# Attention and a gated feed-forward on one core: K and Q rows on every fourth partition, re-timed instruction orders, a shifted end

## The chip, the cores and the metric

The kernel runs on one core of a Trainium2 chip. The metric is the device time of one execution in microseconds. The engines are TensorE (PE, with its weight loads as PEld), VectorE (DVE), ScalarE (ACT), GpSimd (POOL) and the sync engine (SP), which here only issues DMAs.

## The reference

For `x` of 2048 tokens by 448, with 16 heads of width 28 and a hidden width of 1792:

```python
g = sigmoid((x * gate_w).sum(-1, keepdims=True))
# a: attention
q, k, v = split(x @ wqkv)                       # 16 heads, 28 wide
p = softmax(q @ k.T * 28 ** -0.5)
a = concat_heads(p @ v) @ wo
# b: gated feed-forward
gate, up = x @ W_gate, x @ W_up
b = ((gate * (gate > 0)) * up) @ W_down
return g * a + (1 - g) * b
```

All inputs and outputs are float32.

## The kernel before

Most matmuls work in float32r on operands that are split in two, a high part and a low rest (`act_high`, `dve_high` for the first, `low` on VectorE and `pool_low` on GpSimd for the second); products of the parts are added up in PSUM. Eight PSUM banks hold all results of TensorE.

**Projections.** The first 141 us project the tokens to Q, K and V and write them to DRAM (`qk_d`, `v_d`), Q and K as a high and a low plane.

**Heads.** For each head, `load_k` and `load_q` bring K and Q back into one of three buffers each. A buffer stacks four copies of 28 rows (high or low parts), 112 partitions in all, so that one matmul over 128 partitions gives the product of both parts of both sides; the last 16 partitions hold -1 on K's side and the row maxima (as high and low part) or zeros on Q's side. Row maxima are found first: `smax` (line 240) computes scores with queries on the partitions, VectorE takes the maximum (line 241). For three of a head's four blocks of queries (all four of the first head) the probabilities come from `scores` (line 263) with the exponential on ScalarE (line 265). The last block takes another way: `raw_scores` (line 271) copies the scores out, `raw_max` keeps a running maximum over keys, `raw_top` reduces it, writes it to DRAM (`mr_d`) and spreads it back to all partitions, `raw_less` subtracts it on GpSimd and `raw_exp` takes the exponential. `pv` (line 648) multiplies the probabilities with V in 64 matmuls at the end of a round.

**Rounds.** There are 32 rounds, two for each head. Each round's order on TensorE is a string written out ahead: `s` a score matmul, `m` a maximum, `r` a raw score, `x` a matmul of the feed-forward's gate and up part (line 610), each with the bank that it writes as a digit; `d` and `e` stand for a `raw_max` on VectorE and a `raw_exp` on ScalarE. `ROUNDS` lists which string each round uses: FIRST and SECOND for the first head, AA with BA or BB most of the time, DA with BC twice where the feed-forward goes on to another block of tokens, CA, CB, AY, BY, AZ and BZ at the end. A bank can be written again when its reader is done, so the spacing of equal digits in a string sets whether TensorE waits.

At the end of an odd round the sync queue gets, in this order: new blocks of tokens if they change (`X<-x_d`), K of head h+3, the write of `mr_d`, its broadcast (which waits until the write has landed), Q of head h+3, and the next weights of the feed-forward (`wgr<-wgu`). Transfers of one queue are issued in order. The first maximum of head h+3 comes in the following even round.

**Feed-forward.** Gate and up results are multiplied and spilled to DRAM (`h_d`). After the rounds, `down` multiplies them with W_down (line 899): step i reads h of block i, split into `HH` by `split_d`, and the weights `WD` that `split_d` splits too for the first 14 steps. `fetch_d` loads four steps ahead. Between the downs stands the attention's output: `fetch_o` loads the heads' results of a block of tokens into `or` (one buffer), `split_o` splits them in two halves on ScalarE and GpSimd, and `wout` (line 853) multiplies them with `wo`. The list at line 940 says before which down each of these stands.

Of the kernel before, what the change touches and what calls it, by code (L numbers as in the profile page):

```python
# [23 lines left out]
DH = 28  # L24
G = 4
GD = G * DH
# [19 lines left out]

FIRST = ("m2m3m6m7s0s1uxxxxs0xm2lxxs3xm6xUxs1xm7xs0m2xxm3xs1xxs0m7m2s1xr3r0r7m1xdr2xdr3xdxr1s0dxxdxxxm2m0s3xxm"
         "1xm3r2xxm0xdm1xxs3xs0xxm2r3s0m1xdxs2s0m1m2m0m1")  # L50

SECOND = ("xs0m1r2xs6m7dxs3xm0s1xm6s7xr3s2xm1dxs0m7xs6xm2s1r0xs3m6dxs7xm1s2xm3r7xs0xds2m1xs3m0xs7xm2r1s3xm0ds7x"
          "xs2m3xs0r1m2xs3dxm0xs2s3xm1xs2r0m3xs1dm2xxs3m1xs0xs3r2xm1s0dm3xxxs1m0s2xxm1xs2")

AA = ("xm0s1xr2m6s7xm3xs1xm2s7xr0m6xs1dxm3s7xm2xr6s1m0xdxs7m3xs2m1xr0exm7s3dxm2s1exm7xs3xm0er1xs2m3dxes7xm0"
      "xs2m3er1xxs0m2dxes3xxm0m2xes1r3xm0xxdes2m1xs0xem3s2xm1s0xm3r2xs1m0dxxxs1m0")

BB = ("xm0s1r2xm7s6dxxm3s1xm0xs7r6xm2s1dxm3xs0xm7r2s1xm6dxs0xm3xs7m1xr0s2xm3dxs7m1xs2xm3xr7m0s2xdxm1s3xm2s0"
      "xr3xm1s0dxm2xxs1m0s3xxr2m1s3xdm0xxs1m3s2xxm0r1s2m3xdxs0xm2xxs0m1")

BA = ("xs0m1r2s7xm6ds3xs0m1r7xs6m3ds0xr2s1m6xds3xm0s7xr1s6m3s2dxm7s0xr6s3m2xds1m0xs7r3xs2m1ds6xm7s0r2xs1m6d"
      "xs3m0xs7r1s6xm2ds7xm0xs6")

AY = ("xs0m1s2xr6m7s3m0s2xr6xm1s3ds7m2xm0s3xr1s7xm6ds3m2xs0r7s6xm3ds1m0xes2r6xs3m1xem7s2ds0xm1exr3s7m2s6xm0"
      "dexs1m2s7xem6s0xr3xm1s7m2r6ds0xs1m7d")

BY = ("xs0r1ds2xs6xs7xr3ds0s2xs6r1dexs7xs0r2dexs3xs6xs7r1dexs0xs3r2dexxs6r7ds1xs0s3xs2r6ds1xs0xs7xs2s1x")

AZ = ("xs0xs1xxs2xxs6xs7xxs3xs0xxs1xxs2xs7xxs3xs0xxs1xxs2xs3xxs0xxs1xs2exxs3xs0exxs1xxs2exs0xxs1xx")

BZ = ("xs0xs1xxs2xxs6xs7xxs3xs0xxs1xxs2exs7xxs3xes0xxs1xxes2xs3xxs0exxs1xs2xexs3xs0xxs1xxs2xs0xxs1xx")

DA = ("xs0m1xs2r6m7xm3xs0xm2xs6r1m7xs0dxm3xs6m2xr7s0xm1dxs6m3xxm2s0xr1m7s3xdm0xs2xm3xs7m1xr2s0xm7dxs3em1xs0"
      "xm3er2xxs0m1dxem3xs0xm1xes2r0xm3xxdes1m2xs3xm0es1xm2r3xes0m1dxs2xxs1m0m2")

BC = ("xm0s1r2xm7s6dxxm3s1xem0xs7r6xem2s1dxm3xs0exm7r2s1xm6dxs0xm3xs7m1xr0s2xm3dxs7m1xs2xm3xr7m0s2xdxm1s3xm"
      "2s0xr3xm1s0dxm2xxs1m0s3xxr2m1s3xdm0xxs1m3s2xxm0r1s2m3xdxs0xm2xxs0m1")

CA = ("xs0r1m2xs6m7xm3xs0m1xs6m2xr7xs0m3dxm6s1xxm2r0s3xm1dxs7xm6s2xm3xs1m7r0xs2xdm1s3xm7xer2s0xm3dxs1em7xs0"
      "m3xm1exs2m0xxem3r2s1xxdm0exxs3m1s2xexm0r3m2s1xdexs0xm1m2xes3m0xs1xm2xxr0m1s2d")  # L80

CB = ("xs0m1r2s7xm6ds3xm0s1r7exs6m3ds2xem1s0xr3m6s7xs2m1dxes0xr6m7s1xs2m3r0ds7xxm1s3ds2m6xxr7s1m3s0ds2m6xr1"
      "s3xm0ds7xm2s6xr0s7xm1ds6m2xs7")

ROUNDS = [FIRST, SECOND, AA, BA, AA, BB, AA, BA] + [DA, BC, AA, BA, AA, BB, AA, BA] * 2
ROUNDS += [CA, CB, CA, CB, AY, BY, AZ, BZ]

# [13 lines left out]
def gated_mix_kernel(ctx, tc, x, wq, wo, wgu, wd, out):  # L101
    nc = tc.nc
# [9 lines left out]
    def f32(ap):  # L112
        return ap.bitcast(F32)
# [37 lines left out]
    def act_high(dst, src):  # L151
        nc.scalar.activation(dst, src, AF.Copy)  # L152
# [4 lines left out]
    def low(dst, src, high):  # L157
        nc.vector.tensor_tensor(dst, src, f32(high), op=OP.subtract)  # L158
# [5 lines left out]
    qk_d = dram.tile([2, 2 * D, S], F32, name="qk_d")  # L164
# [19 lines left out]
    K = [vp.tile([P, S], F32R, name=f"K{r}") for r in range(3)]  # L184
# [27 lines left out]
    Q = {}  # L212

    def load_k(h):
        for r in range(4):
            nc.sync.dma_start(f32(K[h % 3])[DH * r:DH * (r + 1)], qk_d[r % 2, 2 * DH * h:2 * DH * h + DH, :])

    def load_q(h):
        Q[h] = QB[h % 3].rearrange("p j t -> p (j t)")
        for r in range(4):  # L220
            nc.sync.dma_start(f32(Q[h])[DH * r:DH * (r + 1)], qk_d[r // 2, 2 * DH * h + DH:2 * DH * (h + 1), :])

        n = P - GD if h < 3 else 2
        nc.sync.dma_start(f32(Q[h])[GD:GD + n], z_d[0:1].to_broadcast([n, S]))
# [79 lines left out]
    def xf(tb, b):  # L304
        return X[tb][b // 4][:, b % 4]
# [13 lines left out]
    with tc.tile_pool(name="qkv", bufs=1) as pa:  # L319
# [199 lines left out]
        split_w(*w4)  # L519
        w3 = load_w(3)  # L520
        load_k(0)
        load_q(0)

        units = [(qk, 3, 1), (qk, 2, 2), (qk, 3, 2)]
# [9 lines left out]
        for n, (f, *a) in enumerate(mixed):  # L534
# [3 lines left out]
            if n == 6:  # L538
                load_k(1)
                load_q(1)  # L540
# [5 lines left out]
            if n == len(mixed) - 7:  # L546
                load_k(2)
                load_q(2)
# [30 lines left out]
    done = sum(order.count("x") for order in ROUNDS) // 20  # L579
    SECOND = set(range(1, 2 * done, 2))  # L580
    PAIRED = SECOND | {k - 1 for k in SECOND}

    def lane(k):
        return slice(64 * k, 64 * k + 64)

    def split_f(i, high, low, part=(0, 1)):
# [7 lines left out]
        if part[-1] == 1:  # L594
            high(w[:, :, 6], wr[:, :, 3])
            for s in range(2):
                rows = lane(1 - (2 * i + s in SECOND))
                low(w[rows, s, 6], wr[rows, s, 3], w[rows, s, 6])
# [5 lines left out]
    def gu_mm(ps, i, s, n):  # L604
# [3 lines left out]
        if n == NT - 1 and 2 * i + s in PAIRED:  # L608
            rows = lane(int(2 * i + s in SECOND))
        nc.tensor.matmul(ps, WS[i][rows, s, a], xf(i // NF, b)[rows], start=(n == 0), stop=(n == NT - 1))  # L610
# [93 lines left out]
    for r, order in enumerate(ROUNDS):  # L704
        h, i0 = r // 2, 8 * r
# [15 lines left out]
        for o in re.findall("[a-zA-Z][0-9]?", order):  # L721
# [27 lines left out]
            elif o == "x":  # L749
                i, half, k = todo.pop(0)  # L750
# [124 lines left out]
    WD = pf.tile([P, NF, 2, D], F32R, name="WD")  # L875
# [9 lines left out]
    def split_d(i):  # L885
        if i < NF:
            r = DR.pop(i)
            early = i < 8
            (act_high if early else dve_high)(WD[:, i, 0], r)
            (low if early else pool_low)(WD[:, i, 1], r, WD[:, i, 0])  # L890
        HH[i] = pf.tile([P, 2, TB], F32R, name=f"hh_{i}", tag="hh", bufs=3)
        h = HK.pop(i)
        act_high(HH[i][:, 0], h)
        low(HH[i][:, 1], h, HH[i][:, 0])
# [38 lines left out]
    def before(i, *new):  # L933
        n = todo.index((down, i))
        todo[n:n] = new


    before(3, (normalise, H - 1))
    for tb, load, split, at in ((0, 3, (8, 9), (10, 11, 12, 13)), (1, 8, (12, 14), (17, 18, 19, 20)), (2, 21, (23, 25), (28,) * 4),
                                (3, 35, (37, 39), (42,) * 4)):  # L940
        before(load, (fetch_o, tb))
        for k, i in enumerate(split):
            n = todo.index((down, i))
            n -= todo[n - 1][0] is gate_up
            todo.insert(n, (split_o, tb, 2 * k))
        for t, i in enumerate(at):
            before(i, (wout, tb, t))
# [5 lines left out]
    for n, (f, *a) in enumerate(todo):  # L953
        if n in (7, 8):
            split_d(n - 7)
        if f is down:
            if a[0] + 4 < NB * NF:
                fetch_d(a[0] + 4)
            if a[0] + 2 < NB * NF:
                split_d(a[0] + 2)  # L960
        f(*a)
# [37 lines left out]
```

## Time and profile before

| | us |
|---|---|
| median of 3 executions | 1256.64 (1256.18 to 1258.26) |
| the profiled execution | 1257.98 |
| its span, first to last instruction | 1256.2 |

The profile shows one execution. Its busy time is per engine; matmuls overlap, so TensorE can look busy while it loses time. "line engine out<-in xcount | busy, mean | idle before, who ended it" is the form of a group; a row of the timeline is start, duration, engine, line and operation, with the idle time ahead of it in brackets and what ended it. Rows of SPq are DMA issues, not transfers. A wait that is put down to one DMA can belong to another on the same queue.

### The profile page before, as it was taken

To read this page: it belongs to the slowest core of one execution; us is meant where nothing else is said; L and a number is where in the kernel's file an instruction comes from. 1 tells how busy PE (TensorE), PEld (TensorE's weight loads), DVE (VectorE), ACT (ScalarE), POOL (GpSimd) and SP (SyncE) were. 2 spreads that over 40 slices of the span, in tenths; PEclk is the share of its full clock that TensorE was granted. 3 is DMA by queue.
4 is the path that set the end of the run, shared out by engine and by line. 5 is a ranking of instruction groups with operands and counts; after the bars stand their busy time and mean duration, and the time that the engine had idled before them with its cause. 6 is when DMAs were issued, how large, how long until landed. Compare 5 with 4: busy or idle time off the path is not lost.

```text
span 1256.2 us, 18815 instructions
## 1 busy us (share of the span) xinstructions
PE 1233.8 (98%) x6447; PEld 855.7 (68%) x6447; DVE 897.5 (71%) x1442; ACT 842.5 (67%) x1667; POOL 636.1 (51%) x708
## 2 busy tenths in 40 slices
PE   9999999999999999999999999999999999989998
PEld 6888766666656665666656666665565655989997
DVE  6488879787877877787878787878787734453342
ACT  5312677988788787978787888796877896422121
POOL 4232325573837483838293756646483677551020
PEclk9999999999999999999999999999999999999999
DMA  8986515151544343343535251526241122853432
GB/s 301 306 278 231 183 51 153 51 127 59 135 117 120 95 107 77 101 112 98 145 95 123 78 125 61 133 76 162 59 111 51 52 84 88 272 162 109 147 105 80
DMA packets 62035, 157.64 MB, mean 125 GB/s; under 512 B 12994, under 2 KB 19746, under 8 KB 57514
## 3 DMA queue, kind: packets, MB, share of 16 engines
q1 hardware_dynamic: 47924, 111.47, 32.3%
q0 software_dynamic: 13584, 44.52, 10.1%
q8 instruction: 50, 0.82, 0.3%
q10 hardware_dynamic: 432, 0.46, 0.1%
q14 instruction: 45, 0.37, 0.1%
HBM read 108.70 MB, written 48.16 MB: 125 GB/s over the span
## 4 chain that ended last, share of the span: by engine, by line
PE 72%; DMA 12%; ACT 6%; DVE 3%; POOL 2%; issue 2%; SPq 2%; ACTq 0%; DVEq 0%; POOLq 0%
PE b L610 15%; PE b L648 12%; PE b L240 11%; PE b L263 11%; PE b L899 9%; PE b L434 4%; DMA wgr<-wgu 4%; PE b L271 3%; ACT P L265 3%; PE b L452 3%; PE b L853 3%; DMA mr_d<-V 2%; DMA Q<-qk_d 1%; DMA K<-qk_d 1%; DMA V<-wq 1%
## 5 line engine op out<-in xcount | busy, mean ns | idle before, releaser
L241 DVE TENSOR_REDUCE mx<-b 128x1 f32<-128x512 f32 x784 | 522.9, 687 | 69.9 <-PE b L240 64.7
L265 ACT ACTIVATE P<-b 128x512 f32<-128x512 f32 x780 | 448.8, 608 | 140.1 <-PE b L263 129.5
L610 PE MATMUL b<-X,wg 128*128 128x512 f32 (+1 forms) x1232 | 429.2, 399 | 0.0
L240 PE MATMUL b<-K,Q 128*128 128x512 f32 x784 | 310.7, 400 | 10.9 <-DMA wgr<-wgu 7.3
L263 PE MATMUL b<-Q,K 128*128 128x512 f32 x784 | 312.0, 400 | 2.2 <-ACT P L265 1.9
L610 PEld LDWEIGHTS b<-X,wg 128*128 128x128 f32 (+1 forms) x1232 | 219.6, 188 | 60.7 <-issue 22.2
L648 PE MATMUL b<-P,v 128*32 128x512 f32 x1800 | 226.2, 594 | 0.0
L240 PEld LDWEIGHTS b<-K,Q 128*128 128x128 f32 x784 | 146.1, 188 | 62.9 <-ACT P L265 21.8
L263 PEld LDWEIGHTS b<-Q,K 128*128 128x128 f32 x784 | 147.0, 188 | 54.6 <-ACT P L265 24.2
L632 POOL DMA_DIRECT2D h_d<-rl x56 | 31.5, 564 | 281.2 <-DVE rl L626 234.0
L298 POOL TENSOR_TENSOR P<-P,V 128x512 f32<-128x512 f32 x120 | 150.7, 1291 | 43.4 <-DMA V<-mr_d 43.4
L298 POOL TENSOR_TENSOR V<-V 128x512 f32<-128x512 f32 x120 | 150.8, 1290 | 19.9 <-DMA V<-mr_d 19.9
L161 POOL TENSOR_TENSOR wg<-wgr,wg 128x384 fp32r<-128x384 f32 x216 | 155.5, 734 | 9.6 <-DVE wg L155 1.0
L648 PEld LDWEIGHTS b<-P,v 128*32 128x32 f32 x1800 | 61.7, 110 | 144.5 <-issue 143.4
L279 DVE TENSOR_TENSOR V<-b,V 128x512 f32<-128x512 f32 x215 | 145.9, 679 | 1.8 <-ACT V L275 1.3
L899 PE MATMUL b<-WD,hh 128*128 128x448 f32 x672 | 139.5, 368 | 0.0
L899 PEld LDWEIGHTS b<-WD,hh 128*128 128x128 f32 x672 | 127.5, 190 | 10.3
L152 ACT ACTIVATE hh<-hr 128x512 fp32r<-128x512 f32 x56 | 35.3, 631 | 122.5 <-PE b L899 107.0
L648 PE MATMUL b<-V,v 128*32 128x512 f32 x248 | 110.1, 593 | 0.0
L271 PE MATMUL b<-Q,K 128*128 128x512 f32 x240 | 97.3, 407 | 0.2
L158 DVE TENSOR_TENSOR hh<-hr,hh 128x512 fp32r<-128x512 f32 x56 | 49.2, 880 | 64.3 <-ACT hh L152 64.3
L434 PE MATMUL b<-X,W 128*128 128x512 f32 x280 | 76.0, 395 | 0.6 <-DVE K L158 0.6
(102 smaller groups left out, 1121.5 us busy)
## 6 DMA issues: line engine op xcount, KB each, us to landing
wgr<-wgu SPq DMA_DIRECT2D x55, 512.0 KB
K<-qk_d SPq DMA_DIRECT2D x64, 224.0 KB
Q<-qk_d SPq DMA_DIRECT2D x64, 224.0 KB
h_d<-rl POOLq DMA_DIRECT2D x56, 256.0 KB, 2.9
hr<-h_d SPq DMA_DIRECT2D x56, 256.0 KB
qk_d<-st POOLq DMA_DIRECT2D x21, 512.0 KB, 5.0
X<-x_d SPq DMA_DIRECT2D x24, 256.0 KB
x_d<-X POOLq DMA_DIRECT2D x5, 1024.0 KB, 5.6
```

The lines of the kernel that those rows point to most:

```text
L161: nc.gpsimd.tensor_tensor(dst, src, f32(high), op=OP.subtract)
L240: nc.tensor.matmul(ps, Q[h][:, u * P:(u + 1) * P], K[h % 3][:, c * TB:(c + 1) * TB], start=True, stop=True)
L241: nc.vector.tensor_reduce(MX[h][:, 4 * u + c:4 * u + c + 1], ps, axis=AX.X, op=OP.max)
L263: nc.tensor.matmul(ps, K[h % 3][:, kt * P:(kt + 1) * P], Q[h][:, j * TB:(j + 1) * TB], start=True, stop=True)
L265: nc.scalar.activation(prob(i, j), ps, AF.Exp, scale=SCALE)
L271: nc.tensor.matmul(ps, K[h % 3][:, kt * P:(kt + 1) * P], Q[h][:, 3 * TB:], start=True, stop=True)
L279: nc.vector.tensor_tensor(run, ps, run if i % NK > 1 else prob(i - 1, 3), op=OP.max)
L298: nc.gpsimd.tensor_tensor(own, own, piece(TOP), op=OP.subtract)
L434: nc.tensor.matmul(ps, W[:, a, c * P:(c + 1) * P], xf(tb, b), start=(n == 0), stop=(n == NT - 1))
L610: nc.tensor.matmul(ps, WS[i][rows, s, a], xf(i // NF, b)[rows], start=(n == 0), stop=(n == NT - 1))
L648: nc.tensor.matmul(po[32 * j:32 * j + 32], VH[h][:, i % NK], prob(i, j), start=(i == i0), stop=(i == i0 + ni - 1))
L899: nc.tensor.matmul(ACC[i // NF][t][:, :D], HH[i][:, a, t * P:(t + 1) * P], WD[:, f, b], start=(f == 0 and n == 0), stop=(f == NF - 1 and n ...
```

## The change

Three things change.

1. K and Q rows. Row d of copy r goes to partition 4d + r, where it went to 28r + d. The four transfers for K and for Q stay four, with 28 rows of 8 KB each.
2. Eleven of the thirteen orders are permuted (AZ and BZ are not). Each keeps its number of every letter.
3. The end. `split_d` puts the high part of all fourteen W_down blocks on ScalarE and the low part on VectorE; before, blocks 8 to 13 had their high part on VectorE and the low part on GpSimd. The first block's `split_o` stand before downs 9 and 10 (8 and 9 before) and its four `wout` before downs 12, 12, 13 and 13 (10, 11, 12 and 13 before).

```diff
-AA = ("xm0s1xr2m6s7xm3xs1xm2s7xr0m6xs1dxm3s7xm2xr6s1m0xdxs7m3xs2m1xr0exm7s3dxm2s1exm7xs3xm0er1xs2m3dxes7xm0"
-      "xs2m3er1xxs0m2dxes3xxm0m2xes1r3xm0xxdes2m1xs0xem3s2xm1s0xm3r2xs1m0dxxxs1m0")
+AA = ("xm0s1xr2m6s7xm3xs1xm2s0xr7m6xs1dxm3s0xm2xr6s1xm7dxs0m3xs2m1xr7exm0s2dxm3s1exxm0s2xr7em1s3xdm2xes0xm1"
+      "xs3xexm2r0s1m3xdexs2xm1s3xexm0r2m1s3xdexm0xxs3em1s2xxm0s3xm1s2xm0xxr1s2m0d")
...
     def load_k(h):
+        k = f32(K[h % 3])[:GD].rearrange("(d r) t -> r d t", r=4)
         for r in range(4):
-            nc.sync.dma_start(f32(K[h % 3])[DH * r:DH * (r + 1)], qk_d[r % 2, 2 * DH * h:2 * DH * h + DH, :])
+            nc.sync.dma_start(k[r], qk_d[r % 2, 2 * DH * h:2 * DH * h + DH, :])
 
     def load_q(h):
         Q[h] = QB[h % 3].rearrange("p j t -> p (j t)")
+        q = f32(Q[h])[:GD].rearrange("(d r) t -> r d t", r=4)
         for r in range(4):
-            nc.sync.dma_start(f32(Q[h])[DH * r:DH * (r + 1)], qk_d[r // 2, 2 * DH * h + DH:2 * DH * (h + 1), :])
+            nc.sync.dma_start(q[r], qk_d[r // 2, 2 * DH * h + DH:2 * DH * (h + 1), :])
...
             r = DR.pop(i)
-            early = i < 8
-            (act_high if early else dve_high)(WD[:, i, 0], r)
-            (low if early else pool_low)(WD[:, i, 1], r, WD[:, i, 0])
+            act_high(WD[:, i, 0], r)
+            low(WD[:, i, 1], r, WD[:, i, 0])
...
-    for tb, load, split, at in ((0, 3, (8, 9), (10, 11, 12, 13)), (1, 8, (12, 14), (17, 18, 19, 20)), (2, 21, (23, 25), (28,) * 4),
+    for tb, load, split, at in ((0, 3, (9, 10), (12, 12, 13, 13)), (1, 8, (12, 14), (17, 18, 19, 20)), (2, 21, (23, 25), (28,) * 4),
                                 (3, 35, (37, 39), (42,) * 4)):
```

The other ten changed orders are rewritten in the same way as AA.

More of the change, by code (lines that the diff above doesn't have):

```diff
@@ L43 @@
 AHEAD = 100
[L49 to L53, printed above, removed]
-AA = ("xm0s1xr2m6s7xm3xs1xm2s7xr0m6xs1dxm3s7xm2xr6s1m0xdxs7m3xs2m1xr0exm7s3dxm2s1exm7xs3xm0er1xs2m3dxes7xm0"
-      "xs2m3er1xxs0m2dxes3xxm0m2xes1r3xm0xxdes2m1xs0xem3s2xm1s0xm3r2xs1m0dxxxs1m0")
@@ L58 @@
[L58 to L67, printed above, removed]
+FIRST = ("m2m3m6m7s0s1uxxxxs0xm2lxxxxUs3xxs6s1m7xm0xs2m3xs1m7xxm2xxr0r1r3xm7s2dxr0dxxr7ds2xr1dxr3xs2dxr0dxxxdm"
+         "2s1xm3xxm0s1xm2xm3xm1s0xxm2xm3s0xm1xs2m0m2m1m0")
@@ new lines @@
+SECOND = ("xs0r1m2s6xm7dxs3xs0m2r6xs7m3dxs1xm0xs2m7xs3r1m6xs0xds2xm7xs3m6r0s1xxdm2s7xm3s1xr0s7xm2dxs1m3xs7xm2s1"
+          "xs0r7m3xs1xdm2s0xm3s1xxm0r2xs1s3dxm0xxs1m2s3xm0xs1r2m3xs0xds1xm3xs0m2s1xxxm0s2")
+AA = ("xm0s1xr2m6s7xm3xs1xm2s0xr7m6xs1dxm3s0xm2xr6s1xm7dxs0m3xs2m1xr7exm0s2dxm3s1exxm0s2xr7em1s3xdm2xes0xm1"
+      "xs3xexm2r0s1m3xdexs2xm1s3xexm0r2m1s3xdexm0xxs3em1s2xxm0s3xm1s2xm0xxr1s2m0d")
+BB = ("xs0r1m2xs7m6dxm3xs0xr2s7xm6dxs1m0xm3xs7xm6r1s2xm0dxs7xm3xr2s0m7xds1xm3xm0s7xr1m2xs3dm7xs0xr2m3xs1dxm"
+      "0xxs3m1xs2xxm0r3s1m2xdxs0xxm1s2xm0s3xm1s2xm0r3xm1s2dxs0xxm1m2xs0")
@@ L69 @@
+BA = ("xs0m1r2s7xm6ds3xs0m1r7xs6m3ds0xr2s1m6xds3xm0s7xr1s6m3s2dxm7s0xr6s3m2xds1m0xs7r3xs2m1s6dxm7s0r2xs1m6x"
+      "ds3m0xs7r1s6xm2xds7m0xs6")
+AY = ("xs0m1s2xr6m7s3m0xs2r6xm1s3s7dxm2r0s1xm3ds7xm6s2r1s3xm7xds0m2s6r3xes7m0xds1m6xem2s0xr7s3s1xm6des0m2xs"
+      "3xm6es1xm7em0xs2r3s6xm1r7xds2s0m1m6d")
+BY = ("xs0r1ds2xs6xr7ds3xs0xs2r6ds1exs3xs0r7dexs2s1xxr6des3xs0xs7xr2des1xs6xs3xs0xr7ds2s1s6xxr0dxs2s7s1")
 AZ = ("xs0xs1xxs2xxs6xs7xxs3xs0xxs1xxs2xs7xxs3xs0xxs1xxs2xs3xxs0xxs1xs2exxs3xs0exxs1xxs2exs0xxs1xx")
@@ L71 @@
 BZ = ("xs0xs1xxs2xxs6xs7xxs3xs0xxs1xxs2exs7xxs3xes0xxs1xxes2xs3xxs0exxs1xs2xexs3xs0xxs1xxs2xs0xxs1xx")
[L73 to L80, printed above, removed]
@@ L82 @@
-CB = ("xs0m1r2s7xm6ds3xm0s1r7exs6m3ds2xem1s0xr3m6s7xs2m1dxes0xr6m7s1xs2m3r0ds7xxm1s3ds2m6xxr7s1m3s0ds2m6xr1"
-      "s3xm0ds7xm2s6xr0s7xm1ds6m2xs7")
+DA = ("xs0m1xs2r6m7xxm3s0xm2xs1r6m7xs0xdm3xs2r1m7xs0m6dxxs3m2xs7xm0r3xs1m2dxm7s0xr1xs2xdm0m3xs7m2xs1xem0r7x"
+      "s3m1exds2xm0s3r1xexm2xdm3s0exxm2xxs0em1s3xxm2s0exm1r3xs2em0xds1xxm2s0xm1")
+BC = ("xm0s1r2xm7s6xdxm3s1xem0xs7r6m2exs1xdm3xs0em7xr2xs6m1xds3m0xxm7s1xr3xm2s0dxm1s7xm2xs0xm3r7xs1m0dxs2xm"
+      "3xs1m0xr2xm3s1dxm0xxs3m1xs2xr0m3xs1dm2xxs3xm1s0xm2r3xs1m0dxs2xxs1m0")
@@ L85 @@
+CA = ("xm0s1xr2m6s7xm3xs1m2xs0xr7m6xs1dm3xm0s2xxr6m1s7xdm3xs2xm0s7xr1m2xs3dxm7s0xm2xs3r1m0exs7xdm2xs3em0xr1"
+      "m7xs2em3xds0xxem2xm3s0m1xexs2xr0m3xes1dm2xxs3xem1s0xm2m3xes1m0xs2xxm1xr0s2m1d")
+CB = ("xs0m1r2s7xm6ds3xm0s1r7xes6m3s2dxm1exr0s3m6xs7s2dxm1exr6m3xs7s0s2dm1xr3xs7m6s0xdm2s1xr7s6m0s3dr1xs2xm"
+      "6s0dm3s7xm2s6r0xs7m1xds6xm2s7")
 ROUNDS = [FIRST, SECOND, AA, BA, AA, BB, AA, BA] + [DA, BC, AA, BA, AA, BB, AA, BA] * 2
```

## The prediction, made before the change was run

> **What bounds the kernel now.** I read the page's head first, then who TensorE waited for, then the timeline of one such wait with the sync queue beside it, then windows of the stages.
>
> ```profile
> span 1256.2 us, 18815 instructions
> PE 1233.8 (98%) x6447; PEld 855.7 (68%) x6447; DVE 897.5 (71%) x1442; ACT 842.5 (67%) x1667; POOL 636.1 (51%) x708
> L241 DVE TENSOR_REDUCE mx<-b 128x1 f32<-128x512 f32 x784 | 522.9, 687 | 69.9 <-PE b L240 64.7
> L265 ACT ACTIVATE P<-b 128x512 f32<-128x512 f32 x780 | 448.8, 608 | 140.1 <-PE b L263 129.5
> ```
>
> TensorE is the bound at 98%. That figure hides losses, since a matmul is listed with 0.39 us while the next starts 0.23 us after it (630.01 to 630.24 below). So I look for stretches in which the next start comes later. The waits of TensorE over the whole span:
>
> ```profile
> PE b L240 <- DMA wgr<-wgu: 7.3, 6, 1.8
> PE b L853 <- POOL on L161: 3.3, 1, 3.3
> PE b L263 <- ACT P L265: 1.9, 2, 1.4
> PE b L240 <- DMA Q<-qk_d: 1.8, 2, 1.2
> PE b L240 <- DMA Q<-z_d: 0.7, 1, 0.7
> ```
>
> Nine of these are the same event. L240 is the matmul of the row maxima; it reads K and Q, never wgr. One of the nine, on TensorE and on the sync queue:
>
> ```profile
> 630.01 0.39 PE L263 MATMUL b<-Q,K 128*128 128x512 f32 x1
> 630.24 0.39 PE L610 MATMUL b<-X,wg 128*128 128x512 f32 x1
> 632.30 0.47 PE L240 MATMUL b<-K,Q 128*128 128x512 f32 x1 [1.68 <-DMA wgr<-wgu]
> 632.61 0.40 PE L271 MATMUL b<-Q,K 128*128 128x512 f32 x1
> ```
>
> ```profile
> 602.90 7.22 SPq L614 DMA_DIRECT2D X<-x_d  x8
> 610.17 2.40 SPq L216 DMA_DIRECT2D K<-qk_d  x4
> 615.31 0.31 SPq L293 DMA_DIRECT2D mr_d<-V  x1
> 622.48 0.34 SPq L294 DMA_DIRECT2D V<-mr_d  x1
> 622.87 1.68 SPq L221 DMA_DIRECT2D Q<-qk_d  x4
> ```
>
> Q of head h+3 is issued at 622.87 and its first reader starts at 632.30, 9.4 us later. The queue is late in two ways: the tiny mr_d write (issued 615.31) is known landed only at 622.48, behind X and K, and Q comes behind that. Why Q takes so long is in the windows (us, the engines' busy time, clock, DMA share, GB/s):
>
> ```profile
> 674.00:678.00 4.00, 4.00 (x44) 1.30 (x40) 3.88 (x5) 2.75 (x8) 2.93 (x4) 1.00 0.90 223
> 684.00:690.00 6.00, 6.00 (x28) 4.75 (x26) 5.77 (x10) 5.29 (x10) 3.40 (x3) 1.00 1.02 196
> 691.00:692.50 1.50, 1.06 (x5) 0.93 (x6) 0.91 (x2) 0.26 (x1) 1.50 (x2) 1.00 0.95 371
> Q<-qk_d SPq DMA_DIRECT2D x64, 224.0 KB
> ```
>
> While K (674 to 678) and Q (684 to 690) move, the DMA engines are busy nine tenths of the time or more and carry 196 to 223 GB/s. As soon as wgr, which fills 128 partitions, has them alone, the same share carries 371. So K and Q, written to 28 neighbouring partitions at a time, run at a bit over half rate.
>
> **The change part by part.**
>
> *K and Q rows.* Bytes, descriptors, issues and the place in the queue stay: four transfers of 224 KB each, for K and for Q. Only the partitions differ: 4d+r instead of 28r+d, so each transfer spreads over partitions 0 to 111. The sums over partitions don't care for the order. What the present layout costs: nine gaps, idle 7.3 + 1.8 + 0.7 = 9.8 us, and one wait of 1.4 (L263 on ScalarE), right ahead of a Q wait, which I put down to exponentials on ScalarE that wait for the subtractions of mr_d's broadcast, late for the same reason:
>
> ```profile
> 869.98 0.50 PE L263 MATMUL b<-Q,K 128*128 128x512 f32 x1 [1.39 <-ACT P L265]
> 871.64 0.47 PE L240 MATMUL b<-K,Q 128*128 128x512 f32 x1 [1.16 <-DMA Q<-qk_d]
> ```
>
> Each of these ten ends also costs the overlap of 0.39 - 0.23 = 0.16 and a slow second start (0.31 instead of 0.23, 632.30 to 632.61): 10 x 0.24 = 2.4. Sum 13.6 us. Bounds of the gain: at 371 GB/s the 917 KB of Q take 2.5 us instead of 4.1 to 4.7, which is 1.6 to 2.2 sooner and more than the longest idle of 1.8, so up to all 13.6; if the rate doesn't rise, nothing. A loss is excluded: no transfer is added and 196 GB/s is the slow end already. I take half the step, 1.2 us sooner per load, because the four transfers stay 28 rows each, so they are near to the first two rows in size and near to the third in spread. Then waits under 1.2 go, the ones that have K's landing ahead (mr_d late, as at 615) gain twice, and some 0.6 us remains of the longest; with its end and part of the wait at 870 I leave 2.6 us: gain 11 (0 to 13.6). Late next are the bank waits of the orders (below): VectorE and ScalarE catch up a little while TensorE waits for Q, and no longer would; I take that as covered, as the waits fall early in a round and the readers have P x V at its end to catch up.
>
> The Trainium skill (page "SBUF — State Buffer", section on the DMA port swizzle) says that a run of partitions reaches ports by bits of its number, each worth about 27 GB/s; by it 28 neighbours reach seven ports, an estimate of 190 GB/s, and every fourth partition reaches all sixteen. The trace agrees for the old layout (196 to 223). By that page alone the gain would be the full 13.6.
>
> *New orders.* Every order keeps its counts of each letter, so no matmul is added or lost, and head h+3's first maximum keeps its place in AA after BB or BC and in DA (41 and 60 matmuls into the round), where most Q waits are. Spacing is what moves. Counting in the two sets over all 32 rounds, a bank last read by an exponential is used again five matmuls later 68 times before and once after; six later 164 and 227. For banks read by a maximum, four or five later: 14 and 13. Is that worth much? A bank's cycle is 0.39 + 0.61 us, five matmuls are 1.13: it fits, just. The stage shows where the rest goes:
>
> ```profile
> 260.00:284.60 24.60, 24.53 (x111) 18.36 (x111) 22.75 (x37) 21.84 (x42) 21.14 (x20) 1.00 0.48 114
> ```
>
> The window is a round AA without a Q wait: 99 full matmuls x 0.227 = 22.5, with its half-height ones about 23.1, took 24.6 with VectorE busy for 22.75 and ScalarE for 21.84 (columns three and four after the time). So about 1.3 us of bank waits remain, in a stage where both readers are over 89% busy: an order can smooth queues but not shrink them. AA comes 9 times; BA, 6 times, hardly changes. Bounds: if the nine AA lost nothing any more, -12; if eight rounds lose 1 us more each, +8. The evidence is nearest to a small gain, as the tight reuses vanish but did fit: I take 0.4 in each AA, -3.5.
>
> *The end: outputs two downs later, weights on ScalarE and VectorE.*
>
> ```profile
> 1098.16 2.41 POOL L161 TENSOR_TENSOR on<-or,on 128x1024 fp32r<-128x1024 f32 x1 [4.94 <-ACT on L152]
> 1100.52 1.59 POOL L161 TENSOR_TENSOR WD<-wdr,WD 128x448 fp32r<-128x448 f32 x1
> 1102.07 2.49 POOL L161 TENSOR_TENSOR on<-or,on 128x1024 fp32r<-128x1024 f32 x1
> 1087.17 0.69 DVE L158 TENSOR_TENSOR hh<-hr,hh 128x512 fp32r<-128x512 f32 x1
> 1098.64 2.48 DVE L158 TENSOR_TENSOR hh<-hr,hh 128x512 fp32r<-128x512 f32 x1 [4.56 <-ACT hh L152]
> 1099.15 2.16 PE L853 MATMUL b<-WO,on 128*128 128x448 f32 x9
> 1104.61 0.67 PE L853 MATMUL b<-WO,on 128*128 128x448 f32 x2 [3.30 <-POOL on L161]
> 1104.59 0.38 SPq L830 DMA_DIRECT2D or<-o_d  x1
> 1113.40 0.63 ACT L152 ACTIVATE hh<-hr 128x512 fp32r<-128x512 f32 x1 [13.33 <-DMA hr<-h_d]
> ```
>
> ```profile
> 1105.29 3.99 PE b L899 x12
> 1109.28 2.23 PE b L853 x11
> 1111.50 2.44 PE b L899 x12
> 1104.60:1109.10 4.50, 4.49 (x14) 4.04 (x15) 0.51 (x1) 0.00 (x0) 1.51 (x1) 0.62 0.71 213
> ```
>
> ```profile
> L152 ACT ACTIVATE WD<-wdr x8: 561/563/578, 1071.9 to 1085.3; 128x448 fp32r<-128x448 f32 x8
> L158 DVE TENSOR_TENSOR WD<-wdr,WD x8: 615/619/627, 1072.5 to 1087.8; 128x448 fp32r<-128x448 f32 x8
> ```
>
> Today the first output stops TensorE for 3.3 us (3.5 start to start) while POOL does two splits and a weight between them; after it the granted clock is 0.62 and a down takes 3.99 instead of 2.44, another 1.55. Cost 5.0. The change puts two downs (2 x 2.44) ahead of that output and takes POOL's weight (1.59) out. What is late next: six weights put 6 x 0.56 on ScalarE, idle here, and 6 x 0.62 on VectorE. VectorE's subtractions run 2.48 beside POOL's instead of 0.69 alone, and down 11 is now run ahead of the output: its weight goes behind POOL's first split (to 1101.1), its hh low behind the second (about 1104.1), while TensorE wants it at 1102.0: a wait of 2.1. Then the sync queue: the second block's load of `or` waits until the first is split (issued 1104.59 now, about 1.1 sooner after), and hr of down 12 stands behind it, read at 1113.40 now, at 1112.3 after. Only two outputs instead of three lie ahead of down 12, so TensorE gets there at 1099.15 + 2 x 2.44 + 2.1 + 2 x 2.23 = 1110.6 and waits some 2.4 with the low part. So -5.0 + 2.1 + 2.4 = -0.5, if both waits stay short enough that the clock holds. Ends: -5.0 (VectorE gets in ahead of POOL and hr lands early) and +1.5 (the clock falls again).
>
> The Trainium skill ("SBUF — State Buffer", section on who interferes with whom) says that a VectorE instruction with two SBUF inputs and a GpSimd one that reads SBUF block each other whole; 2.48 against 0.69 agrees, and the rule speaks against giving these weights to VectorE. By it the wait of 2.1 stands; without it the end would gain about 2.6.
>
> **Sum.** -11 - 3.5 - 0.5 = -15. The profiled execution took 1257.98 (span 1256.2), 1.3 over the median of 1256.64, so 1243.0 against it and 1241.6 as a median.
>
> **Rivals.**
> - *The spread rows meet in pairs.* If the DMA engines work in step and every two of them still write into one group of partitions at a time, the rate stays near 200 GB/s and Q lands as before. For it: within a transfer each engine has few rows of 8 KB and no reason to lose step; against: a small offset of starts is enough to undo it, since all groups are used over a transfer. Gain 0 there, total -4: 1252.6. (The Trainium skill, page "DMA: Bandwidth & Descriptors", section on completion counts, would put 28 rows on 14 engines, two rows each, which allows this.)
> - *The orders carry most.* Bank waits fall by 11: total -22.5, 1234.
> - *VectorE becomes the bound.* It is 92% busy in AA. If the new orders bunch the maxima so that one more read of 0.69 is queued on TensorE's path in each of 28 rounds, +19.3 against -11.5: 1264.4, slower. It decides from 0.41 us a round on (11.5 / 28).
> - *Mild form of it*, 0.3 to 0.5 us a round: within 2.5 us of before.
>
> **How the numbers follow.** Within 0.2%, 2.5 us, no change can be told from none here. Forecast 0.57 (its own range 1235 to 1248), pairs 0.15, orders carry most 0.13, mild bunching 0.07, VectorE bound 0.08. Of the pairs case a sixth falls within 2.5 us. So faster 0.57 + 0.13 + 0.125 = 0.83, same 0.09, slower 0.08. The range leaves out the slower case and most of the mild one: 1229 to 1253.
>
> **What would show it.** K and Q: in windows with K or Q alone GB/s over 280 at the same share, and the L240 waits on DMA from 9.8 to under 2 us; unchanged GB/s means the pairs. Orders: AA's stretch ahead of P x V from 24.6 to about 24.1; over 25 with VectorE above 93% means the slower rival. End: no wait of L853 on POOL, instead waits of L899 on hh at about 1102 and 1110 (earlier by what was gained), clock 1.00 throughout. The prediction is wrong if Q lands sooner but another transfer of the same queue takes its place at L240, or if the losses that I call bank waits come from something else.

## The result and the profile after

| | before | after |
|---|---|---|
| median, us | 1258.99 (1256.18 to 1261.09, 6 runs) | 1243.08 (1241.54 to 1246.06, 6 runs) |
| the profiled execution | 1257.98 | 1241.64 |
| its span | 1256.2 | 1239.9 |

The ratio is 0.9877, 95% interval 0.9857 to 0.9897: 15.5 us less (13.0 to 18.0). Forecast were 15. In the kernel after, lines up to L226 moved by one or two and those behind by two (L240 is L242, L263 is L265, L853 is L855); L899 is L900.

The head of the page after:

```profile
span 1239.9 us, 18801 instructions
PE 1228.2 (99%) x6447; PEld 858.5 (69%) x6447; DVE 896.9 (72%) x1442; ACT 842.9 (68%) x1673; POOL 627.5 (51%) x702
```

VectorE and ScalarE are busy as long as before, GpSimd for 8.6 us less (six weights, 8.2 us together, went from it). The span fell because TensorE waits less, so the waits come first, here those of TensorE after (engine, line, what it waited for: us in total, times, longest):

```profile
PE b L900 <- DVE hh L158: 1.4, 1, 1.4
PE b L242 <- DVE mx L243: 1.4, 2, 1.0
PE b L484 <- DVE V L480: 1.2, 1, 1.2
PE b L265 <- ACT P L267: 0.8, 2, 0.6
PE b L900 <- ACT hh L152: 0.8, 1, 0.8
PE b L242 <- ACT P L267: 0.4, 1, 0.4
PE b L612 <- POOL wg L161: 0.3, 1, 0.3
```

No wait of L242 on a DMA is left (9.8 us before), nor one of L855 on POOL (3.3). New are two of L900. The span by stages, cut at the last P x V matmul of each round in the trace. "Q rounds" are the nine even rounds that had a Q wait (2, 6, 8, 10, 14, 16, 18, 22, 24). The first stage is counted from TensorE's first matmul, 1.2 us into the span, so the four stages add up to 1.2 less than the span:

| us | span | round 0 and ahead | nine Q rounds | other rounds | end |
|---|---|---|---|---|---|
| before | 1256.2 | 170.59 | 296.22 | 596.71 | 191.49 |
| after | 1239.9 | 171.38 | 283.56 | 594.50 | 189.23 |
| difference | -16.3 | +0.8 | -12.7 | -2.2 | -2.3 |

How Q came sooner: the sync queue after, in the same round as the prediction's excerpt (issues, not transfers):

```profile
603.69 3.12 SPq L217 DMA_DIRECT2D K<-qk_d  x4
608.81 0.34 SPq L295 DMA_DIRECT2D mr_d<-V  x1
613.80 0.34 SPq L296 DMA_DIRECT2D V<-mr_d  x1
614.19 3.10 SPq L223 DMA_DIRECT2D Q<-qk_d  x4
```

From the mr_d write to its broadcast it takes 5.0 us (608.81 to 613.80), where it took 7.2. This is one of the three rounds that load tokens (7.2 to 7.7 us before, 4.2 to 5.0 after); in the other rounds it takes 1.3 to 2.8 us, before and after. Against the round's start (610.18 after, 616.68 before) Q's issue begins at 4.0 instead of 6.2. And from its first issue to its last row landed, by the transfers' semaphore events, Q takes 7.0 us in the median over heads 3 to 15, before 9.25. Windows while K moves, while Q moves, and behind it with wgr (us, engines' busy time, clock, DMA share, GB/s):

```profile
665.40:669.40 4.00, 4.00 (x40) 1.17 (x36) 3.64 (x5) 3.00 (x8) 2.68 (x4) 1.00 0.84 238
676.00:680.00 4.00, 4.00 (x19) 3.34 (x18) 3.55 (x7) 3.57 (x7) 3.98 (x4) 1.00 0.95 247
680.30:681.80 1.50, 1.50 (x8) 1.25 (x7) 1.50 (x4) 1.48 (x3) 1.50 (x2) 1.00 1.00 396
```

In total that is a rise from 196 to 223 up to 238 to 247, not to the 280 that I had named as the sign. But none of these windows has K or Q quite alone, before or after. Counted by the rows of 8 KB on the sync queue, K carries 179 of the 238 GB/s (before 211 of 223) and Q 160 of the 247 (before 149 of 196); most of what moves beside Q is wgr, 87 GB/s after and 35 before. Over a whole load, from the first row's start to the last row's end (medians of heads 3 to 15), Q's rows pass in 4.4 us instead of 6.5, and K's in 5.5 instead of 5.0. Part of the reason why K gains nothing stands in the issues of K and Q (duration ns min/median/max), before and then after:

```profile
L216 SPq DMA_DIRECT2D K<-qk_d x64: 306/377/1077, 38.5 to 908.9; - x64
```

```profile
L221 SPq DMA_DIRECT2D Q<-qk_d x64: 306/382/1322, 41.0 to 916.7; - x64
```

```profile
L217 SPq DMA_DIRECT2D K<-qk_d x64: 722/732/2528, 37.3 to 896.1; - x64
```

```profile
L223 SPq DMA_DIRECT2D Q<-qk_d x64: 722/732/1659, 40.6 to 903.8; - x64
```

An issue to partitions four apart takes 0.73 us, one to neighbours 0.38. Four take 3.1 us for 917 KB: 296 GB/s at most while they last. K lands no sooner after its first issue than before (7.5 us, before 6.7, medians), but for the three rounds with tokens (9.1 to 9.9 us, before 12.1 to 12.6). A row of 8 KB, of K or Q, takes 436 ns on its DMA engine in the mean, before 570.

Two things changed for Q at once. Its rows lie further apart, and the longer issues put wgr, the next large load on the queue, 3.7 us behind Q's first issue instead of 2.1. In the old layout K's rows, with no such load close behind them, passed in 5.0 us where Q's took 6.5. So up to 1.5 of Q's 2.1 us may come from the later wgr; the old rows with a later wgr were not run.

### The profile page after: what moved, and what is told of

Read it like the earlier page. It is cut to its first block, busy times and chain, and to the rows that moved or that the text cites. A ratio compares the mean times of both kernels' runs of the same rounds, so it can differ in the third digit from the quotient of the medians.

```text
span 1239.9 us, 18801 instructions
## 1 busy us (share of the span) xinstructions
PE 1228.2 (99%) x6447; PEld 858.5 (69%) x6447; DVE 896.9 (72%) x1442; ACT 842.9 (68%) x1673; POOL 627.5 (51%) x702
## 4 chain that ended last, share of the span: by engine, by line
PE 83%; ACT 7%; DMA 3%; POOL 3%; DVE 2%; issue 1%; SPq 0%; DVEq 0%; POOLq 0%; ACTq 0%
PE b L612 17%; PE b L650 16%; PE b L242 13%; PE b L265 12%; PE b L900 9%; PE b L436 6%; PE b L273 4%; ACT P L267 3%; PE b L454 3%; PE b L855 3%; ACT P L304 1%; POOL V L300 1%; ACT V L304 1%; ACT V L277 1%; DVE wg L155 1%
## 5 line engine op out<-in xcount | busy, mean ns | idle before, releaser
L242 PE MATMUL b<-K,Q 128*128 128x512 f32 x784 | 310.6, 399 | 2.8 <-DVE mx L243 1.4
L265 PE MATMUL b<-Q,K 128*128 128x512 f32 x784 | 309.9, 398 | 1.1 <-ACT P L267 0.8
L242 PEld LDWEIGHTS b<-K,Q 128*128 128x128 f32 x784 | 147.0, 188 | 52.5 <-ACT P L267 16.2
L265 PEld LDWEIGHTS b<-Q,K 128*128 128x128 f32 x784 | 146.9, 188 | 48.1 <-ACT P L267 16.4
L900 PE MATMUL b<-WD,hh 128*128 128x448 f32 x672 | 138.3, 366 | 2.2 <-DVE hh L158 1.4
L900 PEld LDWEIGHTS b<-WD,hh 128*128 128x128 f32 x672 | 126.1, 188 | 13.2 <-DVE hh L158 2.2
L277 ACT ACTIVATE V<-b 128x512 f32<-128x512 f32 x116 | 70.1, 609 | 9.6 <-PE b L273 8.7
```

The source lines that it names most:

```text
L242: nc.tensor.matmul(ps, Q[h][:, u * P:(u + 1) * P], K[h % 3][:, c * TB:(c + 1) * TB], start=True, stop=True)
L265: nc.tensor.matmul(ps, K[h % 3][:, kt * P:(kt + 1) * P], Q[h][:, j * TB:(j + 1) * TB], start=True, stop=True)
L277: nc.scalar.activation(own, ps, AF.Copy)
L900: nc.tensor.matmul(ACC[i // NF][t][:, :D], HH[i][:, a, t * P:(t + 1) * P], WD[:, f, b], start=(f == 0 and n == 0), stop=(f == NF - 1 and n ...
```

## The experiments

The first four ran beside one another (kernel before 1257.88), the next four likewise (1259.07), the last two likewise (1258.72). Each ratio is to the kernel before on the same chip.

**Rows alone.** `load_k` and `load_q` as after, all else as before.

> The kernel before with the new K and Q rows alone. Theory (the Q waits carry the change): TensorE's waits for DMA before L240, 9.8 us of idle before, fall under 1 us, and the wait of 1.4 on ScalarE at 870 us goes; time 12 us below the kernel before (10 to 13.5). Rival (the orders carry it, the rows only move the waits to other readers of the same buffers): under 5 us below, with new waits of TensorE at L263 or L271 in the same rounds.

1245.33, ratio 0.9887 (0.9857 to 0.9916): 14.2 us less (10.6 to 18.0), a little more than the 10 to 13.5 expected. Waits of TensorE:

```profile
PE b L855 <- POOL on L161: 2.4, 1, 2.4
```

That one is the longest of them, and none on a DMA is among them. The nine Q rounds take 284.19 (before 296.22): the rows alone take every wait on Q away. The profiled spans differ by 15.4 us; 2.6 of that lie in the end and 0.9 ahead of round 1, which this edit leaves as they were. What the change adds to the rows is small. Whether K's rows, Q's or both are needed was not run.

**Orders alone.** The eleven orders as after, all else as before.

> The kernel before with the new orders alone. Theory: the Q waits stay (8 to 11 us of idle before L240 on DMA) and bank waits fall by 2 to 3 us, so 1 to 4 us below the kernel before. Rival (orders carry the change): 8 us or more below. A third, orders worth less than nothing without the rows, since VectorE and ScalarE catch up during Q waits: 0 to 3 us above.

1257.37, ratio 0.9994 (0.9968 to 1.0021). The interval holds the theory and the third alike; only the rival, orders as the main part, is out. The waits on Q stay, and one is longer:

```profile
PE b L240 <- DMA wgr<-wgu: 10.1, 7, 2.3
PE b L853 <- POOL on L161: 3.5, 2, 3.3
```

A stretch of AA without such a wait, from the round's start to its P x V, is 24.53 us before; with the new order, in the kernel after, and with the old order in the kernel with rows alone:

```profile
259.68:284.07 24.39, 24.32 (x107) 18.27 (x103) 21.82 (x36) 21.64 (x42) 22.02 (x20) 1.00 0.36 114
```

```profile
258.33:282.85 24.52, 24.45 (x107) 18.30 (x104) 22.59 (x37) 21.77 (x42) 22.02 (x20) 1.00 0.39 114
```

AA gains 0.13, where 0.4 was forecast. Orders that I took for neutral gain 0.2 to 0.4 each: SECOND 0.36, BB 0.29, BC 0.3, AY 0.23, BY 0.20 (after against rows alone). CA loses 0.25 to 0.30, and FIRST loses 1.7.

**The end alone.**

> The kernel before with the new end alone (weights on ScalarE and VectorE, first outputs two downs later). Theory: the wait of 3.3 us of L853 on POOL and the slow clock behind it go, waits of 1.4 us (hh of down 11 behind POOL's split) and 0.8 us (hr of down 12 behind the load of or) come: 2 us below the kernel before (1 to 3.5). Rival (end hidden by something that lands at the same time anyway): within 1 us.

1258.71, ratio 0.9991 (0.9969 to 1.0014); the medians' quotient is 1.0007. Neither can be told from 1, so the 2 us expected are neither seen nor excluded. The end takes 188.95 us in the profile, with the two new waits (L898 is L899 of the kernel before):

```profile
PE b L898 <- DVE hh L158: 1.1, 1, 1.1
PE b L898 <- ACT hh L152: 0.7, 1, 0.7
```

The three parts' ratios multiplied, 0.9887 x 0.9994 x 0.9991, give 0.9872, beside 0.9877 for the whole: they add up within their intervals of some 3 us each way, and the rows are nearly all of it.

**Rows two apart.** The four copies go in two pairs, each over 56 partitions, every second one. The lines are shown against the kernel after; orders and end are those of the kernel before.

```diff
-        k = f32(K[h % 3])[:GD].rearrange("(d r) t -> r d t", r=4)
+        k = f32(K[h % 3])[:GD].rearrange("(a d r) t -> a r d t", a=2, r=2)
...
-            nc.sync.dma_start(k[r], ...)
+            nc.sync.dma_start(k[r // 2, r % 2], ...)
```

> The kernel before, with K and Q rows spread half as far: copies 0 and 1 alternate over partitions 0 to 55, copies 2 and 3 over 56 to 111, so a transfer reaches 56 partitions at a step of 2. Theory 1 (what counts is how many neighbours one transfer writes at a time): packets of 8 KB shorten from 570 ns (mean in the kernel before) to near the 436 of the step of 4, Q waits almost gone, 9 us or more below the kernel before. Theory 2 (partitions p and p+32 share a way in, so 56 partitions reach no more of them than 28 or 32): packets stay at 520 to 570 ns. If besides the sync queue issues each transfer in 0.73 us as with the step of 4 (0.38 before), Q lands as late as before or later and the time is within 4 us of the kernel before or above it. If the issue stays at 0.38 us, the long issue belongs to the step of 4.

1245.16, ratio 0.9884 (0.9857 to 0.9912), the same as rows four apart. Of the waits on Q, 0.8 us are left in two, the longer of them here:

```profile
PE b L855 <- POOL on L161: 2.7, 1, 2.7
...
PE b L242 <- DMA Q<-z_d: 0.6, 1, 0.6
```

The mean time of an 8 KB row is 494 ns, between the 570 of neighbours and the 436 of every fourth, so neither of the two values expected; the time is the one that the first theory gave. Q takes 7.9 us to land: 1.35 sooner is enough for nearly all of the gain, since the longest of the Q waits before was 1.8. An issue takes 0.73 us here too, so it is the step between partitions that costs, not its size. With the same issues and with wgr at the same place behind them, Q's rows pass in 5.2 us here and in 4.4 four apart, so these 0.8 us belong to the spread itself.

The Trainium skill ("SBUF — State Buffer", section on the DMA port swizzle) has 28 neighbours on seven ports, 28 rows two apart on eight (copies 0 and 1) or ten (copies 2 and 3), and four apart on sixteen. In proportion to the ports, 570 ns would be an estimate of 499 and 399 two apart, 449 in the mean, and of 249 four apart. The measured 494 and 436 come in this order but stay above 449 and 249, so something else paces these loads too. The issues are a candidate; which it is was not separated.

**Q ahead of mr_d.** Rows as before; Q is issued right behind K, ahead of the mr_d write and its broadcast.

```diff
-        if r % 2 and h + 1 < H:
-            raw_top(h + 1)
...
+        if r % 2 and h + 1 < H:
+            raw_top(h + 1)
```

> The kernel before (old rows, old orders, old end) with Q of head h+3 issued right behind K, ahead of the write of mr_d and its broadcast, instead of behind them. Theory (Q is late for two reasons, its place in the queue and its rate, and either cure removes the waits): Q is issued some 7 to 10 us sooner, TensorE's idle before L240 on DMA falls from 9.8 us to under 1, while the broadcast comes 4 to 5 us later and may make exponentials (ScalarE on POOL) late where tokens are loaded too (3 rounds): 5 to 12 us below the kernel before. Rival (only the rate of the rows counts, the transfers of one queue finish together whatever their order): the waits before L240 stay over 5 us and the time is within 3 us.

1277.18, ratio 1.0137 (1.0095 to 1.018): slower by 17, where 5 to 12 less were expected. All waits of L240 on DMAs are gone, and another takes their place. TensorE's waits, then ScalarE's (1.5 us on this one in the kernel before), then the sync queue and GpSimd in the round shown before:

```profile
PE b L263 <- ACT P L265: 20.4, 14, 4.2
```

```profile
ACT P L302 <- POOL P L298: 16.6, 8, 5.0
```

```profile
620.65 4.30 SPq L221 DMA_DIRECT2D Q<-qk_d  x4
...
627.10 0.31 SPq L293 DMA_DIRECT2D mr_d<-V  x1
634.42 0.34 SPq L294 DMA_DIRECT2D V<-mr_d  x1
```

```profile
639.51 3.74 POOL L298 TENSOR_TENSOR P<-P,V 128x512 f32<-128x512 f32 x3 [12.27 <-DMA V<-mr_d]
```

Read it backwards: the broadcast is issued 7.3 us after the write that it waits for, GpSimd subtracts late, ScalarE stands before an exponential that needs the subtraction, and the exponentials of L265 behind it, which TensorE's banks wait for, are late. Late exponentials were expected in the three rounds with tokens, but TensorE waits over 1 us at L263 in ten: from the mr_d write to its broadcast every round that loads Q now takes 5.2 to 7.5 us, where all but the three with tokens took 1.3 to 2.8. Two small transfers of the queue are as critical as Q. Moving Q ahead of them does not give the gain of the rows; another queue for them was not run.

**The end's places alone.** Splits before downs 9 and 10, outputs before 12, 12, 13, 13; weights as before.

> The kernel before with the new places of the first block's split and outputs alone; the weights of blocks 8 to 13 stay on VectorE and POOL. Theory: the wait of L853 on POOL goes, and hh of down 11 is not late, since VectorE has no weight ahead of it; but POOL's second split comes 1.6 us later behind a weight, the load of or and hr of down 12 behind it too, so the wait before down 12 is 2 to 3 us instead of 0.8: stretch from the end of the rounds 188.5 to 190.5 us. Rival (the weights on POOL are what stops the output, wherever it stands): L853 still waits 1 us or more on POOL.

1259.42, ratio 1.0004 (0.9982 to 1.0027). The end takes 194.61, 4 more than the upper end of what was expected. The wait of L853 on POOL is gone, but the one before down 12 is 3.4 us where 2 to 3 were expected, and the clock is low behind it. TensorE, and then the window behind its wait:

```profile
1111.60 4.51 PE L899 MATMUL b<-WD,hh 128*128 128x448 f32 x12 [3.39 <-ACT hh L152]
```

```profile
1112.00:1116.00 4.00, 3.94 (x13) 3.26 (x13) 3.77 (x6) 2.10 (x3) 3.31 (x2) 0.57 0.47 140
```

**The weights alone.** Blocks 8 to 13 split on ScalarE and VectorE; places as before.

> The kernel before with the weights of blocks 8 to 13 on ScalarE and VectorE alone; split and outputs at their old places. Theory: POOL does its two splits back to back, the wait of L853 falls from 3.3 to 1.7 us and the clock doesn't drop behind it: stretch from the end of the rounds 188 to 190 us (191.5 before). Rival (VectorE's share of the work now blocks POOL's second split): the wait stays over 3 us.

1256.49, ratio 0.998 (0.9955 to 1.0005), the end 187.53, a little under the 188 to 190 expected, and the wait 1.1 where 1.7 was expected:

```profile
PE b L853 <- POOL on L161: 1.1, 1, 1.1
```

Without POOL's weight between its two splits, the wait is 2.2 us shorter. In the profiles, this half of the change at the end does more (187.5) than both together (189.0 to 189.5), but the old end alone differs by more than that from profile to profile (188.9 to 196.1). In the times the intervals of all three overlap.

**A version from these.** The kernel after with the old FIRST and CA, the first block's splits one down apart, and the second block's load two downs later, so that hr of down 12 is not queued behind it.

```diff
-    for tb, load, split, at in ((0, 3, (9, 10), (12, 12, 13, 13)), (1, 8, (12, 14), ...
+    for tb, load, split, at in ((0, 3, (9, 11), (12, 12, 13, 13)), (1, 10, (12, 14), ...
```

> The changed kernel with the old orders FIRST and CA, the first block's second split before down 11 instead of 10, and the second block's load of or before down 10 instead of 8, so that hr of downs 12 and 13 isn't behind it. Theory (FIRST new costs 1.7 us, CA new 0.28 twice, hh of down 11 and hr of down 12 cost 1.4 and 0.8 of wait with their ends): 3 to 5 us below the changed kernel, 0.984 to 0.986 of the kernel before. Rival (the losses are carried over: a shorter first stage or end waits for the same landings): within 1 us of the changed kernel.

1236.8 (1236.41 to 1239.86), ratio 0.9824 (0.9789 to 0.9858), a little lower than the 0.984 to 0.986 expected, with 0.984 inside the interval; the lowest of all medians here. All waits of TensorE over 0.2 us in the whole span, and the stretch around the first outputs:

```profile
PE b L484 <- DVE V L480: 1.2, 1, 1.2
PE b L265 <- ACT P L267: 0.8, 2, 0.5
PE b L436 <- DVE X L158: 0.4, 1, 0.4
PE b L242 <- DVE mx L243: 0.3, 1, 0.3
```

```profile
1074.78 13.13 PE L900 MATMUL b<-WD,hh 128*128 128x448 f32 x64
1087.76 4.62 PE L855 MATMUL b<-WO,on 128*128 128x448 f32 x22
1092.21 2.60 PE L900 MATMUL b<-WD,hh 128*128 128x448 f32 x12
```

The end takes 186.19, 3.0 less than after, and the first round 169.56, 1.8 less.

**The kernel after again, and with the old FIRST alone.**

> The changed kernel once more, on the chip on which the next run stands beside it. Against the kernel before it should give the ratio that it gave at first, 0.9877 (0.986 to 0.990). A wait of L900 on VectorE of 1 to 1.5 us and one on ScalarE of 0.5 to 1 us in the end; no wait of L242 on a DMA.

> The changed kernel with the first round's order put back, all else as changed. My theory, that the new first order loses 1.7 us of what the other orders gain: 1.0 to 2.0 us less than the changed kernel beside it, the stretch up to the end of round 0 at 169.6 instead of 171.4, the later rounds and the end the same within 0.5 us. The rival, that the stretch before round 1 only hands its delay on (round 1 waits for the same things either way): the stretch is shorter, round 1 longer by as much, and the time the same within 0.5 us.

The kernel after: 1244.09, ratio 0.9884 (0.9865 to 0.9903). With the old FIRST: 1242.47, ratio 0.9863 (0.9844 to 0.9882). In the profiles, round 0 ends at 170.08 instead of 171.76, and the later rounds take 877.7 instead of 878.4 together (within 0.5 was expected), so the delay isn't handed on; 1.6 us less in the medians fits, though the two intervals overlap. Over all twelve profiles round 0 ends at 169.6 to 171.0 with the old FIRST and at 171.4 to 171.8 with the new. Another expectation failed: the end of the old-FIRST profile is 2.0 longer (191.57 against 189.52). Its waits are the same two (1.1 and 0.7); over its whole length 50 matmuls start in 10 us instead of 51. Why they do in that one execution stays open.

## Why the prediction was right, step by step

**K and Q rows: -11 forecast, -12.0 (rows alone) to -12.7 (after) in the nine Q rounds.** The waits were the right ones, and they went. That the size is near is in part luck: I priced the ten ends at 13.6 us and left 2.6 standing; none stood, and together they were worth 12.0. Two parts of the reasoning were wrong. "Bytes, descriptors, issues and the place in the queue stay": the issues don't; they last 0.73 instead of 0.38 us. So the rate rose less than the sign that I gave (247, not over 280), and K lands no sooner. Q all the same came 2.3 sooner instead of the 1.2 that I took, and on top of it the mr_d write was known landed 2.2 sooner in the round shown, which is the double gain I had named; it came in the three rounds with tokens alone. The other wrong part is the reading of the windows: I took 684 to 690 for Q alone, but wgr carried 35 of its 196 GB/s and Q's own rows 149. The low rate that I put down to the partitions is in part that of two loads side by side, and how Q's gain divides between the spread rows and the later wgr stays open.

**Orders: -3.5 forecast, about -1.3 in the profiles.** This term was mis-sized. I put 0.4 into each of nine AA and took the rest as neutral. AA gave 0.02 to 0.15 each. The other rounds together gave 2.4 (596.86 with rows alone, 594.50 after), and FIRST, which I did not cost by itself, took 1.7 back, in three short waits of TensorE (on GpSimd's weight split, on a maximum, on an exponential). I had counted bank reuse over all 32 rounds at once, and in such a count an order that is used once can't be seen.

**The end: -0.5 forecast, -2.3 in the profiles.** The steps that I named are all in the trace, with smaller sizes. TensorE, VectorE, GpSimd and ScalarE around the first outputs, after:

```profile
1089.48 2.30 PE L900 MATMUL b<-WD,hh 128*128 128x448 f32 x10 [1.40 <-DVE hh L158]
1097.01 2.23 PE L900 MATMUL b<-WD,hh 128*128 128x448 f32 x8 [0.77 <-ACT hh L152]
```

```profile
1084.18 2.47 DVE L158 TENSOR_TENSOR WD<-wdr,WD 128x448 fp32r<-128x448 f32 x1 [0.72 <-ACT WD L152]
1086.57 2.86 DVE L158 TENSOR_TENSOR hh<-hr,hh 128x512 fp32r<-128x512 f32 x1
```

```profile
1083.76 5.12 POOL L161 TENSOR_TENSOR on<-or,on 128x1024 fp32r<-128x1024 f32 x2 [8.29 <-ACT on L152]
```

```profile
1095.56 0.58 ACT L152 ACTIVATE WD<-wdr 128x448 fp32r<-128x448 f32 x1 [9.95 <-DMA wdr<-wd]
1096.32 0.63 ACT L152 ACTIVATE hh<-hr 128x512 fp32r<-128x512 f32 x1 [0.18 <-PE b L855]
```

Both named waits are there, 1.4 and 0.8 where I had 2.1 and 2.4. (By my own rows the first would have been 2.5: 1099.15 + 2.44 gives 1101.6, not the 1102.0 that I used.) VectorE's weight and hh low each stand beside one of POOL's two splits (2.47 and 2.86, against 0.62 and 0.69 alone), as the prediction had it; the rule of the Trainium skill ("SBUF — State Buffer", section "Who interferes with whom") that a VectorE instruction with two SBUF inputs and a GpSimd one that reads SBUF block each other agrees with this. In the last version, where the splits are one down apart, two weights still take 2.46 and 2.84 us beside them, but a hh low of 0.68 stands between the two, and the wait is gone. The clock stays whole, as forecast:

```profile
1086.00:1090.00 4.00, 2.60 (x14) 2.08 (x13) 3.43 (x2) 0.00 (x0) 2.88 (x2) 1.00 0.03 3
1090.00:1095.00 5.00, 5.00 (x26) 4.65 (x25) 0.00 (x0) 0.00 (x0) 0.00 (x0) 1.00 0.96 282
```

What the term is worth depends on what it is measured against. I took the old end's cost as fixed at 5.0, from one execution. Over the profiles with the old end and new or old rows it took 188.9 (rows alone, wait of 2.4, clock whole), 189.6 (Q ahead of mr_d), 190.5 (rows two apart), 191.5 (before) and 196.1 (orders alone); with the new end 189.0 to 189.5 in three and 191.6 in the fourth. So against the kernel with rows alone the new end gains nothing (189.23 to 188.91).

**The sum: -15 forecast, -15.5 in the medians, -16.3 in the profiled spans.** The terms fit less well than their sum: the orders gave less than half of theirs, and the rows and, in these two profiles, the end gave more. So the close sum is in part luck. A further part that no term holds lies in stretches at half clock, which the last section shows.

**The rivals.** The pairs fell with the first experiment, although the trace has 14 separate landings for each transfer of 28 rows, two rows an engine, as that rival supposed; orders as the main part fell with the second. VectorE did not become the bound: in AA it is busy for 21.82 of 24.39 us, before 22.67 of 24.53.

## What to carry to other kernels

A load that is late by a microsecond or two needs only that much: find its longest wait, then the cheapest layout or place that gives it, and look at what stands behind it on its queue before moving it. Price a rewritten order one string at a time, the first and last ones above all, since those differ from the rest in what they wait for. And a stall's cost taken from one execution should be looked for in a second one before a term is built on it.

## What was not expected of the hardware

**A step between partitions doubles the time of an issue**, from 0.38 to 0.73 us, for a step of two as for four. The first issue of a load, with none just ahead of it, is as long (0.77 to 0.78).

**Waits of about 2 us and more are often followed by a stretch at half clock.** In the kernel with the orders alone, TensorE's wait and the window behind it:

```profile
454.40 0.47 PE L240 MATMUL b<-K,Q 128*128 128x512 f32 x1 [2.31 <-DMA wgr<-wgu]
```

```profile
455.00:460.00 5.00, 5.00 (x17) 3.93 (x16) 3.33 (x6) 4.20 (x8) 5.00 (x5) 0.66 0.32 104
```

A mean clock of 0.66 over 5 us is what 3.4 us at half clock give, and so is the 0.57 over 4 us behind the wait of 3.39 (the end's places alone). In the clock records of all twelve traces every such stretch between the first 25 us and the last matmuls is 3.4 us long, or twice that. Nine of the 14 waits of TensorE of 1.8 us and more have one beside them (1.85, 2.10, 2.12, 2.31, 2.69, 3.30, 3.31, 3.39 and 4.24 us), five have none (1.95, 2.06, 2.28, 2.43 and 3.09), and no shorter wait has one. So the length alone does not decide. The Trainium skill ("TensorE: Matmul & The Clock Gate", section "Why this matters for your kernels") asks for no gaps over about 3 us; five of these nine waits are shorter, and the one of 3.09 has no stretch.

Each stretch of 3.4 us costs 1.7, which is 0.0014 of an execution of the kernel before. That kernel's 57 executions beside the experiments spread over 14.7 us (1252.35 to 1267.08), and their granted clock goes with their time: the 8 at 0.999 or 1.000 took 1255.0 in the mean, the 19 at 0.993 to 0.996 took 1261.7. The kernel after (6 executions beside its variant) was at 0.999 to 1.000 throughout. So a part of the 15.5 us is most likely stretches at half clock that went away with the waits; the prediction counted one of them, at the end. How large that part is was not separated, since only one execution of each kernel has a trace.
